# Holding early loads back until all but the youngest 1.1 MB ahead of them have landed

## The chip, the cores and the metric

One core of a Trainium2 chip runs the whole program in one launch. The metric is the device time of an execution in microseconds. Five engines work side by side, each through its own instructions in order: TensorE (PE in the profile, PEld for its weight loads), VectorE (DVE), ScalarE (ACT), GpSimd (POOL) and SyncE (SP), which issues all loads and stores here.

## What is computed

Attention with two kinds of mask (a local band for half the heads, every 32nd key for the others), and then a gated feed-forward block with a spatial mix over the sequence.

```python
# q, k, v: (8, 8, 576, 64) float32
scores = (1 / np.sqrt(D)) * np.matmul(q, k.transpose(0, 1, 3, 2))
scores = np.where(masks[None], scores, -1e9)       # local for h < 4, strided for the others
attn = softmax(scores)
x = np.matmul(attn, v).transpose(0, 2, 1, 3).reshape(B, S, H * D)   # (8, 576, 512)

h = np.maximum(x @ w_in, 0.0)                      # w_in (512, 1024)
u, v = h[..., :512], h[..., 512:]
v_n = (v - mean(v)) / np.sqrt(var(v) + 1e-6)
v_s = np.einsum('ts,bsd->btd', w_spatial, v_n) + b_spatial[None, :, None]
out = (u * v_s) @ w_out                            # w_out (512, 512)
```

## The kernel before

The kernel works through eight batches. For each, four attention units (two heads each: two local, two strided) make the transposed attention output x; then come the v half of the first product with its normalisation (`moe_1`, line 957), the u half (line 999), the spatial mix (`moe_2`, line 1079, with a tail in lines 1091 and 1092), and the output product as seven smaller products (line 1168). Every operand of a large product is split into a high and a low part and multiplied three times, so weights must be split on the chip before use: a cast on ScalarE, GpSimd or VectorE makes the high part (`rnd`, lines 412 and 414), and a subtraction makes the low one (`rest`, line 422, nearly always VectorE). `w_in` and `w_out` arrive as 8-byte words and are first repaired (`words`: line 789 on ScalarE, 798 on GpSimd, 806 on VectorE). `wsp_sb` is the split spatial weight; `w_out_sb` the split output weight.

All of this is not issued in the order of the code. `Program.add` collects operations with a key, their costs on each engine and what they read and write; `Program.order` is a list scheduler that runs a model of the engines and of the DMA queue and gives each operation an engine and a place; `Program.emit` then issues them in the order of the model's start times. On the chip each engine follows that order strictly and waits for its inputs by semaphores. Between TensorE's real work `emit` puts matmuls on zeros where the model sees a gap (line 1349).

Loads are operations of the engine "sync": `load` (line 440) gives the size in bytes, which `Program.bytes` keeps. A load waits today for the buffer it writes (rings of a few buffers, so for the last reader of what was there before), and the transfers of the queue use eight semaphores in turn, so that it also waits for the one eight places ahead. Early in the program SP's queue holds q, k and v of the first units mixed with the pieces of `w_in`, `w_out` and `wsp`, in the order that the scheduler chose; some pieces borrow buffers that are used for other things later, and the profile names those (`vn<-w_in`, `g<-w_in`, `g<-w_out`, `x<-wsp`, `w_out_sb<-qT`).

Of the kernel before, what the change touches and what calls it, by code (L numbers as in the profile page):

```python
# [61 lines left out]
OTHER_BANK = (1, 2, 3)  # L62
FETCHED, FETCH_COST = 100.0, 32.0
SLOWED = ((0.3, 0.15), (0.45, 0.6), (0.9, 0.8))
DMA_RATE, DMA_ISSUE, DMA_LAG, DMA_TAIL, TABLE_LOAD = 370.0, 470.0, 1500.0, 500.0, 1280.0
PROD = ((0, 0), (0, 1), (1, 0))
BLOCKS = ("a11", "a12", "a22", "s1", "s2", "s3", "s4")
# [4 lines left out]
PE, ACT, DVE, POOL, DMA = "tensor", "scalar", "vector", "gpsimd", "sync"  # L72
# [77 lines left out]
class Program:  # L150
# [39 lines left out]
    def order(self):  # L190
# [17 lines left out]
        def shared(n, e, at, cost):  # L208

            if e in self.port.get(n, ()):  # L210
                since, until, share, _ = held_by[peer[e]]
                if since <= at < until:
                    both = min(until - at, cost)
                    slow = SLOWED[max(share, self.share[n])]
                    return (slow[0] * both, slow[1] * both) if e == DVE else (slow[1] * both, slow[0] * both)
# [115 lines left out]
                free = at + cost  # L331
        return found

    def emit(self, nc, warm):
        issued = self.order()
        fillers = self.fillers(issued)
        for _, n, e in issued:
            if e == PE and fillers.get(n):
                warm(self.spare[n][1], fillers[n])
            self.ops[n][2](getattr(nc, e))  # L340


def pe_cost(m, n):
# [4 lines left out]
def attention_moe(ctx, tc, qT, kT, ks, vl, vs, cst, eye, w_in, w_out, wsp, wtail, out):  # L348
    nc = tc.nc
# [4 lines left out]
    prog = Program()  # L354
# [898 lines left out]
    starts, knots, at = [], [(0.0, NHP)], 0.0  # L1253
# [98 lines left out]
                start=True, stop=True,  # L1352
            )

    prog.emit(nc, warm)


def _layout(q, k, v, w_in, w_spatial, b_spatial, w_out):
# [75 lines left out]
```

## Time and profile before

| | |
|---|---|
| median of 3 runs | 520.41 us (519.15 to 520.59) |
| the profiled execution | 519.78 us, its span 517.7 us |
| granted TensorE clock, mean | 0.98 |
| bytes moved by the data queue | 51.72 MB, 30.3% of 16 DMA engines' span |
| HBM read and written | 42.27 MB and 9.44 MB |
| the chain that ended last | PE 89%, DVE 4%, DMA 2%, ACT 2% of the span |

The span runs from the first to the last instruction of the program; the execution's time is 2.1 us longer. "L422" is line 422 of the kernel; `x<-po` is the tile written and a tile read. In a row of the timeline the first number is the start in microseconds from the start of the span, the second the duration, and square brackets hold the idle time of the engine just before and what ended it. In a row of the DMA issues the last number is the median time from issue to landing.

### The profile page before, as it was taken

Reading aid. Unit: us, or ns where it says so; the run is one execution under the profiler, and the core shown is the slowest. Engines: PE = TensorE matmul, PEld = TensorE weight load, DVE = VectorE, ACT = ScalarE, POOL = GpSimd, SP = SyncE. Lnnn points to the kernel's source line nnn. Section 1 sums busy time; section 2 is a strip of 40 time slices with the busy share of each in tenths; the row PEclk is TensorE's granted clock in tenths of the full one; section 3 lists DMA queues with packets and bytes.
Section 4 is the critical chain, followed back from the end, with each engine's and each line's share of the span. In section 5 each row is a group of like instructions: output and inputs, shape, how many; then the busy total and the mean of one; then the engine's idle time right before and its main releaser. Section 6 shows DMA issues by size and latency. Waiting matters only on the chain.

```text
span 517.7 us, 14663 instructions
## 1 busy us (share of the span) xinstructions
PE 499.6 (97%) x5884; PEld 459.3 (89%) x5884; DVE 363.0 (70%) x1093; ACT 267.4 (52%) x825; POOL 129.0 (25%) x245
## 2 busy tenths in 40 slices
PE   6779889999999999999999999999999999999997
PEld 3558779979999899998999899998999889998997
DVE  2899989969479747896369764897457861676156
ACT  5786765568554476456336276366446252233222
POOL 3355864043212121312102111233102120102000
PEclk9689979999999999999999999999999999999999
DMA  8897323454024322262023422063011300020002
GB/s 274 307 343 268 125 83 90 149 164 151 2 79 151 118 79 81 85 180 84 11 69 121 148 80 80 1 209 113 1 56 53 123 1 1 1 80 13 1 1 91
DMA packets 26243, 52.65 MB, mean 102 GB/s; under 512 B 3136, under 2 KB 11584, under 8 KB 26176
## 3 DMA queue, kind: packets, MB, share of 16 engines
q1 hardware_dynamic: 26176, 51.72, 30.3%
q8 instruction: 46, 0.75, 0.6%
q14 instruction: 21, 0.17, 0.1%
HBM read 42.27 MB, written 9.44 MB: 100 GB/s over the span
## 4 chain that ended last, share of the span: by engine, by line
PE 89%; DVE 4%; DMA 2%; ACT 2%; SPq 1%; POOL 1%; issue 1%; POOLq 0%
PE m L1079 20%; PE m L957 18%; PE m L1168 18%; PE m L999 18%; PE po L720 4%; PE po L617 3%; PE s L507 3%; PE s L650 2%; PE m L1091 2%; PE m L1092 2%; DMA k<-kT 1%; SPq L442 1%; DMA x<-wsp 1%; PE po L1349 1%; DVE w_in_sb L422 0%
## 5 line engine op out<-in xcount | busy, mean ns | idle before, releaser
L1079 PE MATMUL m<-wsp_sb,vn 128*128 128x288 f32 x768 | 113.3, 300 | 4.3 <-DVE wsp_sb L422 4.3
L1079 PEld LDWEIGHTS m<-wsp_sb,vn 128*128 128x128 f32 x768 | 107.3, 192 | 5.4 <-DVE wsp_sb L422 4.6
L999 PE MATMUL m<-x,w_in_sb 128*128 128x288 f32 x768 | 105.3, 297 | 0.0
L999 PEld LDWEIGHTS m<-x,w_in_sb 128*128 128x128 f32 x768 | 103.4, 188 | 1.2
L957 PE MATMUL m<-w_in_sb,x 128*128 128x512 f32 (+1 forms) x408 | 99.5, 399 | 0.0
L957 PEld LDWEIGHTS m<-w_in_sb,x 128*128 128x128 f32 (+1 forms) x408 | 74.5, 186 | 19.0 <-DVE x L422 0.2
L1168 PE MATMUL m<-g,w_out_sb 128*128 128x288 f32 x384 | 56.9, 298 | 0.0
L414 POOL TENSOR_SCALAR ptl<-pc 32x64 f32<-32x64 f32 (+3 forms) x89 | 37.9, 426 | 64.7 <-DVE pc L588 24.2
L1168 PEld LDWEIGHTS m<-g,w_out_sb 128*128 128x128 f32 x384 | 52.3, 188 | 1.0 <-ACT vv L434 0.3
L422 DVE TENSOR_TENSOR x<-po,x 128x288 fp32r<-128x288 f32 x64 | 27.6, 447 | 36.3 <-ACT x L434 35.6
L1101 DVE TENSOR_TENSOR u<-m,u 128x288 f32<-128x288 f32 x64 | 28.1, 453 | 30.9 <-PE m L1092 30.7
L564 ACT ACTIVATE pl<-pl,ml 128x64 f32<-128x64 f32 (+1 forms) x140 | 47.0, 339 | 4.7 <-DVE ml L544 4.3
L915 ACT ACTIVATE vv<-m 128x512 f32<-128x512 f32 (+1 forms) x37 | 22.0, 596 | 45.7 <-PE m L957 39.6
L412 ACT CAST g<-u 128x288 fp32r<-128x288 f32 x46 | 19.2, 434 | 50.2 <-DVE u L1101 49.0
L933 POOL TENSOR_TENSOR bn<-bn,sel 128x1 f32<-128x1 f32 (+1 forms) x37 | 21.1, 575 | 95.0 <-DVE bn L928 77.0
L1013 ACT ACTIVATE u<-m 128x288 f32<-128x288 f32 x64 | 25.7, 408 | 35.0 <-PE m L999 34.6
L1168 PE MATMUL m<-vn,w_out_sb 128*128 128x288 f32 x288 | 42.6, 297 | 0.0
L920 DVE BATCH_NORM_STATS2 bn<-vv 128x6 f32<-128x512 f32 (+1 forms) x37 | 25.3, 683 | 21.0 <-ACT vv L915 20.5
L1168 PEld LDWEIGHTS m<-vn,w_out_sb 128*128 128x128 f32 x288 | 39.5, 188 | 0.4
L434 ACT CAST x<-po 128x288 fp32r<-128x288 f32 x64 | 24.7, 397 | 26.2 <-PE po L617 14.4
L412 ACT COPY ptl<-pc 32x64 f32<-32x64 f32 (+3 forms) x103 | 35.7, 346 | 4.7 <-DVE pc L588 2.6
L422 DVE TENSOR_TENSOR g<-u,g 128x288 fp32r<-128x288 f32 x64 | 27.0, 449 | 7.9 <-ACT g L412 6.2
(131 smaller groups left out, 726.6 us busy)
## 6 DMA issues: line engine op xcount, KB each, us to landing
q<-qT SPq DMA_DIRECT2D x30, 295.0 KB, 4.2
outT<-o SPq DMA_DIRECT2D x48, 144.0 KB, 2.7
v_raw<-vs SPq DMA_DIRECT2D x13, 512.0 KB, 4.2
v_raw<-vl SPq DMA_DIRECT2D x16, 384.0 KB, 3.7
k<-kT SPq DMA_DIRECT2D x16, 304.0 KB, 4.5
kbd<-ks SPq DMA_DIRECT2D x32, 144.0 KB, 4.6
outT<-vv SPq DMA_DIRECT2D x16, 144.0 KB, 3.7
vn<-w_in SPq DMA_DIRECT2D x4, 512.0 KB, 4.5
```

Source lines behind the costliest of these rows:

```text
L412: eng.copy(dst(), src())
L414: eng.tensor_scalar(dst(), src(), 1.0, 0.0, op0=ALU.mult, op1=ALU.add)
L422: eng.tensor_tensor(dst(), src(), f32(hi()), op=ALU.subtract)
L434: eng.copy(dst(), src())
L564: eng.activation(p_sb()[:m, u, :], src, AF.Exp, bias=st()[:m, u : u + 1], scale=SCALE if masked else -1.0, **total,)
L920: lambda eng: eng.bn_stats(bn()[:m, 0:6], v()[:m]), [(v,)], [(bn,)],
L957: eng.matmul(v_ps()[:m, :], x_at(kt)[:, a, :], w_in_sb[:, w, kt, HF:], start=(n == 0 and i == 0), stop=(n == NT - 1 and i == 2),)
L999: eng.matmul(u_ps()[:, :HS], w_in_sb[:, w, kt, f * P : (f + 1) * P], xs[NHP * b + kt]()[:, a, r], start=(n == 0 and i == 0), stop=(n == NT ...
L1013: lambda eng, u=u, f=f, u_ps=u_ps: eng.activation(u()[:, f * HS : (f + 1) * HS], u_ps()[:, :HS], AF.Relu),
L1079: eng.matmul(s_ps()[:, :HS], vn()[:, a, kt, fs], wsp_sb[:, w, kt, r], start=(kt == 0 and i == 0), stop=False,)
L1101: lambda eng, ug=ug, s_ps=s_ps: eng.tensor_tensor(ug(), s_ps()[:, :HS], ug(), op=ALU.mult),
L1168: eng.matmul(o_ps()[:, :HS], w_out_sb()[:, b_at, w, kk, a * P : (a + 1) * P], at(j, kk), start=first and kk == 0 and i == 0, stop=kk == 1 ...
```

## The change

While `emit` issues the operations it keeps a list of the transfers whose modelled start lies before `GATE_END`. For each it counts bytes back from itself, its own included, as long as they fit in `GATE`, and makes it wait until the transfer just ahead of those has landed. SP takes its instructions in order, so whatever stands behind a waiting transfer waits with it. The order of all engines is what it was.

```diff
+GATE, GATE_END = 1.1e6, 70000.0
...
-    def emit(self, nc, warm):
+    def emit(self, nc, warm, wait):
         issued = self.order()
         fillers = self.fillers(issued)
-        for _, n, e in issued:
+        sent = []
+        for at, n, e in issued:
             if e == PE and fillers.get(n):
                 warm(self.spare[n][1], fillers[n])
-            self.ops[n][2](getattr(nc, e))
+            made = self.ops[n][2](getattr(nc, e))
+            if e == DMA and at < GATE_END:
+                sent.append((made, self.bytes[n]))
+                under_way, k = 0, len(sent)
+                while k and under_way + sent[k - 1][1] <= GATE:
+                    k -= 1
+                    under_way += sent[k][1]
+                if 0 < k < len(sent):
+                    wait(made, sent[k - 1][0])
...
-    prog.emit(nc, warm)
+    def wait(later, earlier):
+        tc.add_manual_dep(
+            later.ins if hasattr(later, "ins") else later, (earlier.ins if hasattr(earlier, "ins") else earlier).name,
+            mybir.DependencyInfo(mybir.DependencyClass.Sync, mybir.DependencyReason.DATA),
+            reason="transfers under way",
+        )
+
+    prog.emit(nc, warm, wait)
```

The first 57 transfers of SP's queue fall under it, all of them loads. Here they are in the order of the queue, with the source, the size in KB, and behind ">" the transfer that each now waits for:

```
#0 qT 295 | #1 vs 512 | #2 cst 96 | #3 eye 64 | #4 w_in 512 >1 | #5 ks 144 >1
#6 ks 144 >1 | #7 qT 295 >4 | #8 kT 304 >4 | #9 vl 384 >6 | #10 qT 295 >7 | #11 kT 304 >8
#12 vl 384 >9 | #13 w_in 512 >11 | #14 w_in 512 >12 | #15 qT 295 >13 | #16 ks 144 >13 | #17 ks 144 >14
#18 vs 512 >15 | #19 qT 295 >16 | #20 w_in 512 >18 | #21 ks 144 >18 | #22 ks 144 >19 | #23 w_in 512 >20
#24 w_in 512 >22 | #25 vs 512 >23 | #26 ks 144 >24 | #27 ks 144 >24 | #28 w_in 512 >25 | #29 qT 295 >26
#30 kT 304 >28 | #31 vl 384 >28 | #32 w_in 512 >30 | #33 qT 295 >31 | #34 kT 304 >32 | #35 wsp 288 >32
#36 w_out 512 >34 | #37 kT 304 >35 | #38 qT 295 >36 | #39 ks 144 >36 | #40 ks 144 >36 | #41 vs 512 >38
#42 wsp 288 >39 | #43 w_out 512 >41 | #44 wtail 288 >42 | #45 vl 384 >43 | #46 qT 295 >43 | #47 kT 304 >44
#48 wtail 288 >45 | #49 wsp 288 >46 | #50 wsp 288 >47 | #51 w_out 512 >49 | #52 w_out 512 >50 | #53 vl 384 >51
#54 qT 295 >52 | #55 ks 144 >52 | #56 ks 144 >52
```

## The prediction

> **What bounds the kernel now.** I read the page's header first, then stretches of time, then the chain that ended last, then the engines' timelines around the last place where TensorE starves, and only then the DMA queue. The number of a transfer (#0, #1, ...) is its place in SP's queue, as in the list under "The change".
>
> ```profile
> span 517.7 us, 14663 instructions
> PE 499.6 (97%) x5884; PEld 459.3 (89%) x5884; DVE 363.0 (70%) x1093; ACT 267.4 (52%) x825; POOL 129.0 (25%) x245
> ```
>
> TensorE is busy for 97% of the span. The view of stretches says where the missing 18 us lie (per row: stretch, its length, then busy time and instructions of PE, PEld, DVE, ACT and POOL, the granted TensorE clock, DMA share, GB/s):
>
> ```profile
> 10.00:20.00 10.00, 6.07 (x158) 3.66 (x160) 6.90 (x20) 5.17 (x20) 2.15 (x4) 0.53 1.01 389
> ...
> 50.00:60.00 10.00, 10.00 (x93) 9.91 (x78) 10.00 (x22) 8.18 (x27) 9.13 (x12) 1.00 0.65 228
> 60.00:70.00 10.00, 5.72 (x25) 4.34 (x24) 9.50 (x31) 8.53 (x32) 7.65 (x9) 0.76 0.30 105
> ...
> 80.00:517.00 437.00, 434.16 (x4921) 406.19 (x4919) 297.91 (x930) 210.85 (x663) 83.62 (x172) 1.00 0.24 78
> ```
>
> From 80 us on PE is idle for 3 us in 437: whatever delays the point at which PE becomes saturated delays the end by as much. The chain that ended last names that point (a piece of VectorE work, just ahead of PE's), and the timelines of PE and DVE show both sides of it:
>
> ```profile
> 65.82 1.35 DVE wsp_sb L422 x2
> ```
> ```profile
> 67.21 3.01 PE L1079 MATMUL m<-wsp_sb,vn 128*128 128x288 f32 x11 [4.28 <-DVE wsp_sb L422]
> ```
> ```profile
> 40.19 0.69 DVE L806 SCALAR_TENSOR_TENSOR vn<-vn 128x512 int32<-128x512 int32 x1
> ...
> 53.36 1.17 DVE L806 SCALAR_TENSOR_TENSOR g<-g 128x512 int32<-128x512 int32 x1
> ...
> 65.75 2.08 DVE L422 TENSOR_TENSOR wsp_sb<-x,wsp_sb 128x576 fp32r<-128x576 f32 x3
> ```
>
> PE waits 4.28 us for the last part of wsp_sb, and VectorE is why: it is busy for all 10.00 us from 50 to 60 and for 9.50 of the next ten, in a fixed order. What it does at 53.36 (the word repair of #43, a piece of w_out) is therefore tied to the end: 67.21 - 53.36 = 13.85 us of VectorE work, then 450.5 us of PE work. A microsecond of delay at 53.36 is one at the end. What feeds that instruction is a transfer, through ScalarE:
>
> ```profile
> 51.88 0.70 ACT L789 ACTIVATE g<-g 128x512 f32<-128x512 f32 x1
> ```
>
> **How the transfers run now.** SP's timeline (issue, then the time the issue takes), and the times from issue to landing (rows of narrow windows of the DMA view; the last number of each):
>
> ```profile
> 1.17 0.42 SPq L442 DMA_DIRECT2D xt<-vs  x1
> ...
> 7.59 0.43 SPq L442 DMA_DIRECT2D k<-kT  x1
> 8.07 0.43 SPq L442 DMA_DIRECT2D v_raw<-vl  x1
> ...
> 16.19 0.33 SPq L442 DMA_DIRECT2D g<-w_in  x1
> ...
> 45.60 0.36 SPq L442 DMA_DIRECT2D g<-w_out  x1
> ```
> ```profile
> k<-kT SPq DMA_DIRECT2D x1, 304.0 KB, 6.1
> v_raw<-vl SPq DMA_DIRECT2D x1, 384.0 KB, 8.1
> g<-w_in SPq DMA_DIRECT2D x1, 512.0 KB, 7.3
> g<-w_out SPq DMA_DIRECT2D x1, 512.0 KB, 6.3
> ```
>
> #11 (k) lands at 13.7, #12 (v_raw) at 16.2, #20 (g<-w_in) at 23.5, #43 at 51.9. #20 is issued just as #12 lands, eight places back: eight transfers under way is the limit now, some 2.9 MB there. They land in the order of their issue, while the engines are full (DMA share 1.01, 389 GB/s from 10 to 20 us). So 7 or 8 us to landing is queueing that hides the fixed part of a transfer's time. Loads issued into an empty or nearly empty queue show that part:
>
> ```profile
> w_out_sb<-qT SPq DMA_DIRECT2D x1, 295.0 KB, 3.0
> xt<-vs SPq DMA_DIRECT2D x1, 512.0 KB, 3.8
> kbd<-ks SPq DMA_DIRECT2D x2, 144.0 KB, 2.4
> vn<-w_in SPq DMA_DIRECT2D x1, 512.0 KB, 4.2
> k<-kT SPq DMA_DIRECT2D x1, 304.0 KB, 3.6
> xt<-vs SPq DMA_DIRECT2D x1, 512.0 KB, 3.7
> g<-w_out SPq DMA_DIRECT2D x1, 512.0 KB, 3.5
> g<-w_out SPq DMA_DIRECT2D x1, 512.0 KB, 4.4
> ```
>
> These are #0, #1, #21 and #22, #23, #37, #41, #51 and #52. At some 400 GB/s (the 389 above, rounded) 512 KB take 1.3 us and 300 KB 0.8 us; the rest, 2.2 us at the least for the large ones, does not depend on size.
>
> **The change, part by part.** It adds one wait to nearly every one of the first 57 transfers and moves nothing. The wait is on SP, in order: behind a waiting load stand all later loads, whichever engine needs them. The issue itself costs no more. Per wait the price is this: with own bytes counted in the 1.1 MB, a 512 KB load may go out only when at most 0.58 MB is still under way, often one load. Those bytes drain in some 1.4 us, and the new load lands no sooner than 3.5 us after its issue, so the queue runs dry between them.
>
> I followed the rule through the list of sizes. A gated load is issued when the load named lands, and lands a hop later; where the load ahead of it in the queue is later still, it lands a transfer time behind that one. The longest path to #43 is #1, 4, 7, 8, 11, 13, 15, 18, 20, 23, 25, 28, 30, 32, 34, 36, 38, 41, 43. Each arrow but 7 to 8 (queueing, 0.8 us) is a gate: eleven hops with 512 KB (4, 13, 18, 20, 23, 25, 28, 32, 36, 41, 43) and six with about 300 KB (7, 11, 15, 30, 34, 38). #1 lands at 1.17 + 3.77 = 4.9.
>
> - Low end: the fixed part from the 144 KB row, 2.4 - 0.4 = 2.0, so hops of 3.3 and 2.75. #43 lands at 4.9 + 36.3 + 16.5 + 0.8 = 58.5.
> - High end: the slowest rows, 4.4 and 3.6: 4.9 + 48.4 + 21.6 + 0.8 = 75.7.
> - Taken: 3.7 for 512 KB (the row of #41, issued behind two small ones, is nearest to the gated state) and 3.3 for 300 KB (the middle of 3.0 and 3.6): 4.9 + 40.7 + 19.8 + 0.8 = 66.2, against 51.9 now.
>
> The sum hangs on the fixed part: 0.1 us of it is 1.7 us of the answer, which makes the range wide. A gain is excluded on this path: landings follow the order of issue, the order stays, and no issue comes earlier.
>
> The Trainium skill has a price of its own: "DMA: Bandwidth & Descriptors", section "Anatomy of one DMA — SWDGE (gpsimd) path", gives a DMA about 2.0 us fixed and its bytes over 436 GB/s besides (3.2 and 2.7 us for these sizes, for transfers that GpSimd issues). By that #43 would land at 57.1 and the kernel take 525 us; the trace's eight rows all lie above it, so the rows decide.
>
> From #43 to the end: landing 66.2, ScalarE's 0.70, a handover of 0.15, so L806 starts at 67.05 in place of 53.36: **+13.7 us**. The 13.85 us of VectorE work behind it then run as now.
>
> What else could be late is covered. #32 lands at 48.5 by the same hops; its L806 then starts near 49.3 instead of 40.19, and 13.2 us of VectorE work (53.36 - 40.19) bring #43's turn to 62.5, 4.5 us before its data. If that cover is gone (VectorE slower by more), VectorE's order sets the end and the rest adds up. The last wsp load, #50, waits for #47 and lands near 74; the split that uses it on VectorE, now at 65.75, comes at 79.4, and a cast of about 0.7 stands between, so over 4 us cover it. #51 and later loads wait for buffers that the delayed work frees, and move with it. PE has 4.28 us of starvation before wsp_sb today and will have more; its saturated stretch behind is unchanged.
>
> Sum: 517.7 + 13.7 = 531.4 of span; the profiled execution took 519.78, 2.1 more than its span, so 533.5. The median of the runs, 520.41, lies 0.6 above that execution: **534.1, say 534 us**.
>
> **The rivals.**
>
> 1. *Hidden for the most part (522.5 to 525.5).* Later loads wait for buffers anyway:
>
> ```profile
> 22.09 1.12 SPq L442 DMA_DIRECT2D kbd<-ks  x2
> ...
> 33.63 0.38 SPq L442 DMA_DIRECT2D g<-w_out  x1
> ```
>
> If these waits set the pace, only the start slips: by the hops #11 lands at 4.9 + 3.7 + 3.3 + 0.8 + 3.3 = 16.0 against 13.7, +2.3, which gives 522.7, and up to twice that with #12 and #13. Against it: #21 to #36, sixteen loads, now go out within 11.5 us; by the gates #36 goes out six hops (23, 25, 28, 30, 32, 34: 21.4 us) after #20 has landed. 0.08.
>
> 2. *Faster (519).* TensorE stalls once early with nothing in the profile to wait for, in the stretch where the queue is deepest:
>
> ```profile
> 16.39 0.46 PE L507 MATMUL s<-k,q 64*32 64x64 f32 x13 [1.45 <-issue]
> ```
>
> If that is code that arrives late because the same 16 engines are full, a shallow queue gives back up to 1.45 us: 520.4 - 1.45 = 519. It decides only if the hops cost nothing, that is, if 1.1 MB keeps the engines full, which needs a fixed part under 1.3 us (the two 512 KB loads that 1.1 MB admits take 2.6 us, less one load's own 1.3); no row is near that. The skill's same page, section "Queues, rings and completion order", says that an engine takes turns between queues packet by packet, by which a deep data queue would hold code up little; the one stall cannot tell. 0.04.
>
> 3. *The wait is not there (520.4).* The transfers already share eight semaphores in turn, and a wait that the program thinks implied could be dropped. In the list nearly every gate names a load two to four places back, which the eight-deep rule does not imply. 0.06.
>
> 4. *Dearer (above 543).* If a hop with one load ahead is always like #52 (4.4) or VectorE's cover goes as well: 544 and more. 0.06.
>
> **How the numbers follow.** The forecast, 525.5 to 543, has 0.76: its ends are the low end (58.5, that is +6.0, 526.4, and up to 1 us back where VectorE shares less with GpSimd) and just under the high end (75.7 gives +23.2, 543.6). With rival 1 the range 522.5 to 543 holds 0.84. Slower by over 0.3% (1.6 us, about what a measurement here can tell from no change): 0.76 + 0.08 + 0.06 = 0.90; within 0.3%: 0.06; faster: 0.04.
>
> **What would show it.** Right: loads up to #50 take 3 to 4.5 us to land instead of 5 to 9; SP's waits are on DMAs, two to four loads back; the DMA rate from 10 to 60 us is near 230 GB/s (#7 to #40, 11.6 MB) without stretches at 390; #43 lands between 59 and 76; VectorE idles before L806 until its load; the first L1079 batch starts near 81 and the distance from there to the end is still 450 us. Wrong: loads land as late after issue as now (no wait); the hops are shorter than 3.3 us (#43 before 58, gain in the fixed part); L806 at its present place relative to VectorE's earlier work (something else sets the pace); or PE's later stretch changes length.

## The result and the profile after

The changed kernel takes 534.89 us (median of 6 runs, 532.01 to 535.14); the kernel before took 519.14 in the 6 runs beside it (517.61 to 520.59). The ratio is 1.0287, with a 95% interval of 1.0255 to 1.0319: slower by 15.7 us. The profiled execution took 534.91 us, and its span was 532.9, against 519.78 and 517.7.

The code below the new lines has moved: L806 of before is L816 after, L422 is L432, L1079 is L1089. The header of the page after:

```profile
span 532.9 us, 14663 instructions
PE 503.6 (95%) x5884; PEld 461.3 (87%) x5884; DVE 357.7 (67%) x1093; ACT 266.3 (50%) x825; POOL 128.7 (24%) x245
```

The instructions are the same in number; VectorE's busy time even fell by 5 us. Stretches of time, in the same columns as before (PE, PEld, DVE, ACT, POOL, granted clock, DMA share, GB/s):

```profile
10.00:20.00 10.00, 4.63 (x211) 3.43 (x212) 6.11 (x16) 4.11 (x15) 1.07 (x3) 0.56 0.82 247
...
40.00:50.00 10.00, 6.53 (x120) 5.21 (x121) 4.57 (x10) 2.13 (x5) 1.80 (x3) 0.94 0.70 229
50.00:60.00 10.00, 6.27 (x31) 5.04 (x29) 5.77 (x31) 4.33 (x10) 3.77 (x5) 0.84 0.58 189
60.00:70.00 10.00, 9.41 (x142) 8.81 (x143) 5.08 (x11) 5.97 (x22) 4.29 (x9) 0.71 0.72 224
...
90.00:532.00 442.00, 439.43 (x5033) 411.09 (x5031) 302.85 (x941) 214.09 (x674) 86.72 (x179) 1.00 0.24 78
```

Two things changed. The queue that moved 389 GB/s from 10 to 20 us moves 247 there and 189 to 229 in the later rows shown. Over the whole stretch from 10 to 60 us, before and then after:

```profile
10.00:60.00 50.00, 42.44 (x711) 35.02 (x712) 45.37 (x113) 36.06 (x107) 27.53 (x43) 0.86 0.81 290
```
```profile
10.00:60.00 50.00, 32.68 (x595) 24.46 (x595) 30.94 (x88) 25.09 (x70) 15.80 (x28) 0.78 0.71 222
```

And VectorE, which was full from 50 us on, is idle for half of the time from 40 to 70. From 90 us on PE is as saturated as it was from 80 on before.

The chain that ended last (start, length, what; the pieces of SP and of issue, 0.02 to 0.4 us each, are left out here) is at first a file of transfers, one released by another:

```profile
1.16 4.83 DMA xt<-vs
...
6.01 3.49 DMA vn<-w_in
...
9.89 3.21 DMA k<-kT
...
13.12 4.22 DMA k<-kT
...
17.36 3.69 DMA u<-w_in
...
58.75 2.75 DMA q<-qT
...
61.57 3.50 DMA xt<-vs
...
65.15 3.72 DMA g<-w_out
...
68.92 3.10 DMA v_raw<-vl
...
72.09 3.46 DMA x<-wtail
...
75.57 0.67 ACT wt_b L422
```

These are #1, 4, 8, 11, 13, then 38, 41, 43, and behind them #45, #48 and ScalarE's cast of what #48 brought. Between #13 and #38 the chain holds #15, 18, 20, 23, 25, 28, 30, 32, 34 and 36. Up to #43 this is the path that the prediction followed through the list of sizes, but for #7: the chain goes from #4 straight to #8, since both wait for #4. The prediction did not have #45 and #48. On VectorE and PE, from the repair of #32 on:

```profile
51.92 0.69 DVE L816 SCALAR_TENSOR_TENSOR vn<-vn 128x512 int32<-128x512 int32 x1 [3.80 <-POOL vn L808]
...
69.66 0.69 DVE L816 SCALAR_TENSOR_TENSOR g<-g 128x512 int32<-128x512 int32 x1 [3.71 <-POOL g L808]
...
73.67 0.55 DVE L950 TENSOR_SCALAR vv<-vv,bn 128x512 f32<-128x512 f32 x1 [0.45 <-POOL bn L943]
...
76.79 0.88 DVE L432 TENSOR_TENSOR vn<-vv,vn 128x512 fp32r<-128x512 f32 x1 [0.36 <-ACT vn L422]
...
81.80 2.08 DVE L432 TENSOR_TENSOR wsp_sb<-x,wsp_sb 128x576 fp32r<-128x576 f32 x3
```
```profile
83.27 7.81 PE L1089 MATMUL m<-wsp_sb,vn 128*128 128x288 f32 x47 [3.01 <-DVE wsp_sb L432]
```

VectorE stands idle for 3.71 us in front of the repair of #43 (GpSimd's half of the repair, L808, is named, and that waited for the load), and again 3.80 us in front of that of #32. The repair of #43 starts at 69.66 instead of 53.36, and PE's first batch with the full wsp_sb at 83.27 instead of 67.21. Between the two VectorE stands idle twice more, for 0.45 us and for 0.36. The second is the place where the chain joins it: ScalarE's cast of `vn` came behind its cast of #48, which was late. What this is worth the run upto43 tells.

### The profile page after: what moved, and what is told of

The parts are those of the page before. It is cut to its first block, busy times and chain, and to the rows that moved or that the text cites. A ratio compares the mean times of both kernels' runs of the same rounds, so it can differ in the third digit from the quotient of the medians.

```text
span 532.9 us, 14663 instructions
## 1 busy us (share of the span) xinstructions
PE 503.6 (95%) x5884; PEld 461.3 (87%) x5884; DVE 357.7 (67%) x1093; ACT 266.3 (50%) x825; POOL 128.7 (24%) x245
## 4 chain that ended last, share of the span: by engine, by line
PE 84%; DMA 14%; DVE 1%; ACT 0%; SPq 0%; issue 0%
PE m L1089 20%; PE m L1178 17%; PE m L967 17%; PE m L1009 17%; PE po L627 3%; PE po L730 3%; DMA k<-kT 3%; DMA vn<-w_in 2%; PE s L517 2%; PE s L660 2%; PE m L1101 2%; PE m L1102 2%; DMA xt<-vs 2%; DMA u<-w_in 1%; DMA g<-w_out 1%; DMA v_raw<-vs 1%
## 5 line engine op out<-in xcount | busy, mean ns | idle before, releaser
L1089 PE MATMUL m<-wsp_sb,vn 128*128 128x288 f32 x768 | 112.4, 298 | 3.0 <-DVE wsp_sb L432 3.0
L1089 PEld LDWEIGHTS m<-wsp_sb,vn 128*128 128x128 f32 x768 | 106.5, 191 | 4.1 <-DVE wsp_sb L432 3.3
L1009 PE MATMUL m<-x,w_in_sb 128*128 128x288 f32 x768 | 106.5, 298 | 0.7 <-ACT vv L925 0.6
L967 PE MATMUL m<-w_in_sb,x 128*128 128x512 f32 (+1 forms) x408 | 102.5, 408 | 1.6 <-ACT u L1023 1.6
L967 PEld LDWEIGHTS m<-w_in_sb,x 128*128 128x128 f32 (+1 forms) x408 | 76.5, 191 | 21.4 <-ACT u L1023 1.8
L432 DVE TENSOR_TENSOR x<-po,x 128x288 fp32r<-128x288 f32 x64 | 27.6, 449 | 40.5 <-ACT x L444 39.9
L422 ACT CAST g<-u 128x288 fp32r<-128x288 f32 x46 | 19.1, 434 | 50.3 <-DVE u L1111 49.2
L422 ACT COPY ptl<-pc 32x64 f32<-32x64 f32 (+3 forms) x103 | 35.6, 346 | 4.3 <-DVE pc L598 2.3
L444 ACT CAST x<-po 128x288 fp32r<-128x288 f32 x64 | 24.6, 398 | 23.0 <-PE po L627 13.7
L950 DVE TENSOR_SCALAR vv<-vv,bn 128x512 f32<-128x512 f32 (+1 forms) x37 | 21.5, 580 | 18.9 <-POOL bn L943 18.5
```

What stands on the lines that cost most here:

```text
L422: eng.copy(dst(), src())
L432: eng.tensor_tensor(dst(), src(), f32(hi()), op=ALU.subtract)
L444: eng.copy(dst(), src())
L967: eng.matmul(v_ps()[:m, :], x_at(kt)[:, a, :], w_in_sb[:, w, kt, HF:], start=(n == 0 and i == 0), stop=(n == NT - 1 and i == 2),)
L1009: eng.matmul(u_ps()[:, :HS], w_in_sb[:, w, kt, f * P : (f + 1) * P], xs[NHP * b + kt]()[:, a, r], start=(n == 0 and i == 0), stop=(n == NT ...
L1089: eng.matmul(s_ps()[:, :HS], vn()[:, a, kt, fs], wsp_sb[:, w, kt, r], start=(kt == 0 and i == 0), stop=False,)
```

## The experiments

Three theories. *Round trip*: each transfer costs some 2.2 to 2.6 us that do not depend on its size; 1.1 MB under way is too little to cover them, the queue falls to about half its rate wherever waits stand, and the end follows #43. *Start*: only the first loads cost, and all the rest is their delay carried on. *Waits*: the added waits cost time on SP, by their number. All experiments are the changed kernel with one or two lines different; ratios are to the kernel before on the same chip.

**Another size: 2.0, 1.6 and 0.8 MB.**

```diff
-GATE, GATE_END = 1.1e6, 70000.0
+GATE, GATE_END = 2.0e6, 70000.0     # gate20; gate16: 1.6e6; gate08: 0.8e6
```

> GATE 2.0e6 in place of 1.1e6, all else as changed: nearly as many loads wait, each for one further back. Round trip (too few bytes under way for the fixed part of a transfer): 2.0 MB are 5 us at 400 GB/s, longer than a hop of some 3.8 us, so the engines never run dry and the time is that of the kernel before, 519 within 0.3% (517.5 to 521); #43 lands near 52. Waits (each added wait costs SP time): most of the 16 us stay, 530 or more. A shallow queue that helps code to arrive: 518 or less, and the 1.45 us stall of TensorE near 15 us is gone.

Measured: 517.85 us, ratio 0.9977 (0.9958 to 0.9996); #43 lands at 49.8. The waits theory falls: by the list of sizes 50 of the 57 loads still have a wait (53 in the changed kernel), and nothing is lost. The queue keeps its rate: 290 GB/s from 10 to 60 us, the figure of before, against 222 in the changed kernel. This is slightly faster than before, which the last two experiments take up.

> GATE 1.6e6. Round trip: the hops just about keep the engines busy; followed through the list with a fixed part of 2.5 us, #43 lands 2 us later than before (near 54) and the time is 521 (519 to 523.5). Waits: as with 1.1 MB, near 534.

Measured: 519.37, ratio 1.0020 (1.0002 to 1.0038); #43 lands at 52.6, 0.8 us after its landing before; VectorE waits for it again, but only 0.84 us. The knee lies where the round trip puts it; the time was put 1.6 us too high.

> GATE 0.8e6: behind a 512 KB load only one of 144 to 272 KB may be under way. Round trip: the same path through the list gives #43 at about 101, L816 at 102, so 567 (555 to 575), three times the loss of 1.1 MB. Start (only the first loads cost): the first k and q come some 6 us later than with 1.1 MB, 541. Waits: near 534.

Measured: 561.16, ratio 1.0806 (1.0781 to 1.0832); #43 lands at 93.4 and its repair starts at 94.12. The start theory (541) and the waits theory (534) both fall. The round trip has the direction and seven eighths of the size: it said +48, measured +42. The step that was off is the fixed part, which I had raised to 2.5 us after the changed kernel. With less under way most of the large loads land sooner again; three rows of narrow windows of this kernel's DMA view (#43, #24, #36):

```profile
g<-w_out SPq DMA_DIRECT2D x1, 512.0 KB, 3.5
g<-w_in SPq DMA_DIRECT2D x1, 512.0 KB, 3.5
g<-w_out SPq DMA_DIRECT2D x1, 512.0 KB, 3.4
```

**Waits on a part of the queue.**

```diff
# early
-GATE, GATE_END = 1.1e6, 70000.0
+GATE, GATE_END = 1.1e6, 22000.0
# late
-                if 0 < k < len(sent):
+                if 0 < k < len(sent) and at >= 22000.0:
```

> Waits only on the first 25 loads (#0 to #24). Start: the whole loss is there, 534. Round trip: #24 lands near 37 as in the changed kernel against 29 before, then the ungated queue runs at 400 GB/s and makes up part; #43 lands at 54 to 58, and the time is 522 to 526.

> Waits only from #25 on; the first 25 loads go out as before. Start: no loss, 519. Round trip: eight hops from #25 to #43 still stand in the chain; #43 lands near 60.5 against 52 before and 69 changed, L816 at 61.4, so 527 (524 to 530).

Measured: early 524.78, ratio 1.0118 (1.0094 to 1.0143), #43 lands at 56.2; late 527.04, ratio 1.0140 (1.0118 to 1.0161), #43 lands at 59.8. Each half of the waits costs part, 5.6 and 7.3 us, and together they make 13 of the 15.7. The start alone is not it: with the first 25 loads as before, the later waits still open the gap. In the late kernel VectorE waits for the load, as in the changed one:

```profile
60.59 0.69 DVE L816 SCALAR_TENSOR_TENSOR g<-g 128x512 int32<-128x512 int32 x1 [3.62 <-POOL g L808]
```

In the early one it does not, although the repair is 6.4 us late. There the freed queue has caught up, and what is late is VectorE's own order: the chain that ended last in this kernel goes through #32, which landed at 46.2 (38.0 before), and VectorE's work behind it:

```profile
59.80 0.67 DVE L816 SCALAR_TENSOR_TENSOR g<-g 128x512 int32<-128x512 int32 x1
```

**Which load is tied to the end.**

```diff
-GATE, GATE_END = 1.1e6, 70000.0
+GATE, GATE_END = 1.1e6, 34500.0     # upto36; upto43: 40500.0
```

> Waits on #0 to #36 alone; #37 to #43 go out as soon as their buffers allow. Round trip with the end tied to #43: #36 lands near 58.5 as in the changed kernel, the next seven loads (2.4 MB) stream and #43 lands near 64 in place of 69; VectorE's own order from #32 on allows L816 no earlier than 65, so 530 (528.5 to 531.5), about 4.5 less than the changed kernel. If the end is not tied to #43: 534 to 535.

> Waits on #0 to #43 alone; #44 to #56 (wtail, the last wsp, q, k and v of later units, w_out) are free. Cover as predicted: #43 lands as in the changed kernel, the loads behind it come up to 3 us earlier and nothing gains by it, 534 to 535. If the later loads, wtail or wsp above all, set the end: 1 us or more faster, 533.5 or less.

Measured: upto36 529.12, ratio 1.0186 (1.0164 to 1.0208), #43 lands at 63.7; upto43 534.36, ratio 1.0280 (1.0247 to 1.0314), with #50 landing at 74.5, 3 us earlier than with all waits. Freeing the seven loads up to #43 brings some 5 us; freeing all behind it brings nothing that can be told from zero. That holds for #48 too: in upto43 ScalarE's cast of it starts at 73.06 instead of 75.57, VectorE's idle time of 0.36 us is gone, and from the repair of #43 to PE's first full batch it still takes 13.64 us, against 13.61. In upto36 VectorE waits for the load by 0.37 us only, so that its own order is close to taking over, as the cover said:

```profile
64.49 0.69 DVE L816 SCALAR_TENSOR_TENSOR g<-g 128x512 int32<-128x512 int32 x1 [0.37 <-POOL g L808]
```

Over all runs the tie is plain. The last column is the span less the start of #43's repair:

| kernel | #43 lands | its repair starts | span | from there to the end |
|---|---|---|---|---|
| before | 51.9 | 53.4 | 517.7 | 464.3 |
| gate20 | 49.8 | 52.2 | 515.4 | 463.2 |
| gate16 | 52.6 | 53.4 | 517.3 | 463.9 |
| early | 56.2 | 59.8 | 522.6 | 462.8 |
| late | 59.8 | 60.6 | 523.9 | 463.3 |
| upto36 | 63.7 | 64.5 | 528.9 | 464.4 |
| upto43 | 67.6 | 68.4 | 533.3 | 464.9 |
| changed | 68.9 | 69.7 | 532.9 | 463.2 |
| gate08 | 93.4 | 94.1 | 559.3 | 465.2 |
| g20early | 48.6 | 51.3 | 514.9 | 463.6 |
| g20late | 51.0 | 54.0 | 518.0 | 464.0 |

The start moves by 43 us and the rest stays within 2.4. VectorE waits for #43 itself in the changed kernel, gate16, gate08, late, upto36 and upto43; in the other kernels its own order decides when the repair starts.

**Where the small gain of 2.0 MB lies.** In gate20 the early stall of TensorE, 1.45 us before, was 0.40. The matmuls ahead of the stall before, and then those around it in gate20:

```profile
13.82 1.12 PE L507 MATMUL s<-k,q 64*32 64x64 f32 x59 [1.27 <-DMA k<-kT]
```
```profile
13.89 1.12 PE L517 MATMUL s<-k,q 64*32 64x64 f32 x59 [1.24 <-DMA k<-kT]
15.41 0.46 PE L517 MATMUL s<-k,q 64*32 64x64 f32 x13 [0.40 <-issue]
```

The k of #11 lands at the same time (13.76, before 13.68), and PE stops after the same 59 matmuls. Both traces record one 16 KB packet of an instruction queue there, which starts at 13.21 instead of 14.16. It is put down to PE because PE restarts 2.2 to 2.4 us after its start in each of the five traces that have the stall (before, gate20, gate16, late, g20late). So the 2.0 MB were tried on each half of the queue:

```diff
# g20early
+GATE, GATE_END = 2.0e6, 22000.0
# g20late
+GATE, GATE_END = 2.0e6, 70000.0
+                if 0 < k < len(sent) and at >= 22000.0:
```

> GATE 2.0e6, waits on #0 to #24 only. With 2.0 MB the code for TensorE that is fetched near 14 us came 1 us earlier than before (stall 0.40 against 1.45 us) and the kernel was 0.23% faster. If that gain is the early code: stall again near 0.4 us, VectorE's L816 of #43 about 1 us earlier than before (52.2 against 53.4), and 518 (0.997 to 0.999 of before). If it comes from the later loads, or is chance: 519, ratio 1.000.

> GATE 2.0e6, waits on #25 to #56 only. Early code theory: the stall of TensorE near 15 us is that of before, 1.4 to 1.6 us, L816 of #43 near 53.4, and the time is that of before, 519 (ratio 0.999 to 1.001). If the gain of 2.0 MB comes from later: ratio 0.998 and L816 near 52.2 with the stall in place.

Measured: g20early 517.72, ratio 0.9968 (0.9952 to 0.9984); g20late 519.08, ratio 0.9994 (0.9979 to 1.0010). PE's timelines, of g20early and then of g20late:

```profile
14.19 1.33 PE L517 MATMUL s<-k,q 64*32 64x64 f32 x72 [1.20 <-DMA k<-kT]
```
```profile
13.59 0.80 PE L517 MATMUL s<-k,q 64*32 64x64 f32 x59 [2.12 <-DMA k<-kT]
16.35 0.46 PE L517 MATMUL s<-k,q 64*32 64x64 f32 x13 [1.96 <-issue]
```

With the early waits all 72 matmuls run in one piece; without them the stall is there, 1.96 us. The gain is in the early part as far as the intervals tell, which still overlap a little, and g20early is the kernel here that is most clearly faster than before, by 0.3%. That the stall is all of the gain isn't shown: #43's repair starts at 51.27 there, 2.1 us earlier than before, and the stall was 1.45. No run took the stall away by itself. Single executions also scatter: gate20 has the same waits as g20early on #0 to #24, and yet its packet starts at 13.21 and that of g20early at 11.98.

All eleven traces together are clearer. In the three kernels without early waits (before, late, g20late) the packet starts 3.0 to 3.6 us after PE's first matmuls on the new k (`m<-k,q`); in the eight with them it starts 0.3 to 1.9 us after.

## Why the prediction was right

*What bounds.* The tie from #43's repair to the end held in every run (the table). The stretch on VectorE behind it took 83.27 - 69.66 = 13.61 us, against 13.85 before, but it was not the same stretch. Before, VectorE was busy throughout; after, it was idle for 0.81 us (0.45 and 0.36), and its operations took 1.1 us less (the repair 0.69 instead of 1.17). Two differences that the prediction did not have cancel here, which is luck.

*The price of a wait.* Right as a mechanism and as a path: the queue moves 222 GB/s where it moved 290, and up to #43 the chain has the hops that were named. Only the step from #4 to #8 went without #7; it took 3.6 us, for 4.1 taken.

*The sizes.* The hops came to 68.87 - 5.99 = 62.9 us, for 61.3 taken (40.7 + 19.8 + 0.8), on average 2.5 us above the transfer time instead of 2.4 and 2.5 for the two sizes. That average holds the queueing behind the one or two loads that were let out ahead as well; the runs don't separate the two. #1 landed at 5.99 and not at 4.9; no added wait stands ahead of it, and in the other kernels where none does it landed between 4.9 and 6.5, so that is scatter. Together #43 was 2.7 us later than forecast. The shift was +16.3 at VectorE, for 13.7. The Trainium skill's price ("DMA: Bandwidth & Descriptors", section "Anatomy of one DMA — SWDGE (gpsimd) path", 2.0 us and 436 GB/s), which gave 525, was too low for these loads from SP's queue; the rows were right to decide.

*What gave a little back.* From PE's restart to the end were 449.6 us, not 450.5. The first 47 matmuls took 7.81 us instead of 8.65, at a higher granted clock. The first five microseconds around the restart and the five after, before and then after the change (clock ahead of the DMA share):

```profile
65.00:70.00 5.00, 2.79 (x11) 2.79 (x12) 4.50 (x12) 4.93 (x24) 4.38 (x3) 0.53 0.61 210
70.00:75.00 5.00, 5.00 (x32) 5.00 (x32) 4.85 (x8) 2.16 (x4) 2.79 (x3) 0.79 0.01 3
```
```profile
80.00:85.00 5.00, 1.99 (x9) 1.74 (x8) 4.99 (x24) 4.88 (x21) 4.68 (x5) 0.79 0.69 198
85.00:90.00 5.00, 5.00 (x36) 5.00 (x35) 4.58 (x10) 2.92 (x10) 3.36 (x4) 0.87 0.05 15
```

So the span grew by 15.2 us where 13.7 were forecast. That the 534 stands so near the 534.89 is partly luck: the kernel before measured 519.14 over six runs, 1.3 less than the median that the sum started from, and this offset most of the 2 us by which the change itself was put too small.

*The cover.* #32's repair came at 51.92 (forecast 49.3), and VectorE still stood idle for 3.71 us before #43's, for 4.5 of cover. #50 landed at 77.6 (forecast 74) with the split at 81.80. It was enough, as upto43 shows. The cover of #48 (wtail) was not looked at, and it fell short by 0.36 us; upto43 shows that this, too, did not set the end.

*The rivals.* "Hidden for the most part" fell with late: ring waits did not pace the later loads. "The wait is not there" fell with the chain. "Faster" was wrong for 1.1 MB for the reason given, but the traces bear its mechanism out: with early waits the packet of code starts earlier. The rule set beside it was that engines take turns between queues (same page of the Trainium skill, section "Queues, rings and completion order"), by which a deep data queue would hold code up little. The traces do not agree: without early waits the packet starts 3.0 to 3.6 us after PE's first matmuls on the new k, with them 0.3 to 1.9.

## What to carry to other kernels

A limit on the bytes under way is a limit on the rate: no more than the bytes allowed, divided by the time from issue to landing. Take that time from a load in a nearly empty queue (3.5 us for 512 KB here, not the 7 or 8 of a full one), and look for the bytes at which it equals the time they take to move: 3.5 us at 400 GB/s are 1.4 MB. Stay above that. The rate falls short of the quotient (222 GB/s measured, where 1.1 MB in 3.7 us would be 297), because only whole loads go out and they seldom fill the allowance, which is argued and not tested. Here 2.0 MB cost nothing, 1.6 MB 0.2%, 1.1 MB 3% and 0.8 MB 8%. Then find the load whose landing is tied to the end, because the price is read there. It need not be the same one in every variant: here it was #43, and #32 where only the first loads had waits.

## What was not expected of the hardware

- Loads that are held back early let TensorE's code in earlier. PE stood still for 1.45 to 1.96 us near 15 us in the three kernels without early waits; with 2.0 and 1.6 MB it was 0.40 and 0.56, and in g20early there was no stall. What in the queue holds the packet of code up isn't shown.
- The time of a load that is alone in the queue is not one number. With 0.8 MB a 512 KB load often goes out when all ahead of it have landed: #13, 20, 24, 25, 36 and 43 then took 3.4 to 3.6 us, but #32 took 4.30, and why isn't shown. In the changed kernel, with one or two others under way, 512 KB loads among #4 to #43 took 3.46 to 4.98 us.
